# Chunked attention and token mixer on one core: stores on two queues and a new hand-ordered list

## The chip, the cores and the metric

The kernel runs on one core of a Trainium2 chip. The metric is the device time of one execution in microseconds (us). The kernel before takes 140.97 us (median of 3 runs, 140.26 to 141.21). One more execution was taken with the hardware profiler: it took 141.5 us, and its span, from the first to the last instruction of the program, is 139.7 us.

## The reference

Two layers follow each other. The first is attention inside chunks of 64 tokens (8 batches, 8 heads, 576 tokens of 64 values, so 9 chunks per head). The second is a token mixer without a softmax on the result, x, of the first.

```python
scores = scale * q_c @ k_c.T            # per chunk of 64 tokens and per head
attn   = exp(scores - max); attn /= sum + 1e-9
x      = (attn @ v_c)                   # -> [8, 576, 512]
wq, wk = x @ w_q, x @ w_k               # 512 -> 64
W_tok  = 1/8 * einsum('bsd,btd->bst', wq, wk)
mixed  = einsum('bst,btd->bsd', W_tok, x)
out    = relu(mixed) @ w_out            # float32 [8, 576, 512]
```

The kernel uses that `mixed = wq @ (wk.T @ x)`: it forms the small matrix G = wk.T @ x of a batch (64 x 512) and multiplies it with wq, so that no 576 x 576 matrix is made.

## The kernel before

**Units.** The tokens are cut into 20 units (`pairs`, lines 139 to 143). A whole unit has 256 tokens of one batch; a rest unit (u2, u7, u12, u17) has the last 64 tokens of two neighbouring batches. Units 18 and 19 are the two whole units of batch 7, unit 15 and 16 those of batch 6.

**Nodes.** Each unit goes through the same steps, each a `Node`: transposes of q and k on TensorE (`tq`, line 380), their copies out of PSUM (`qkt`: into `qbd` for q and `kt` for k), the scores S (line 400), maximum, subtraction and exponential (lines 413, 424, 434), transposes of the exponentials (line 446), attention times V (line 477), division (lines 491 to 505, giving `xs`), transposes of x (line 523), projections to wq and wk (line 533, `wt`), a transpose of wk (line 550). When both units and the rest of a batch are there, G follows (line 587, copied to `g16`), then for each unit the mix (line 627), the relu (`rm`, lines 645 and 647) and the output products (line 662), whose results are copied to `osb` in SBUF (line 313, through the helper `copy`) and stored to HBM. A copy out of PSUM can go to VectorE or ScalarE.

**The order.** Nothing is scheduled on the chip. `ORDER` (lines 69 to 104) is a list made offline, by a planner with costs for each node and landing times for each load. `12a` runs node 12 on ScalarE, `12v` on VectorE, `12p6` on TensorE with PSUM bank 6, and `i7.256` is an idle product: a product of ones with 256 columns into bank 7 (line 701) that nobody reads. The list is emitted from left to right (lines 697 to 706); each engine runs its own instructions in the order of emission and waits for semaphores where a node needs another one's result.

**Loads and stores.** The q and k of the first unit come by SyncE's queue as float32 (line 205) and are cast by four `cast` nodes, 0 to 3. All other loads are issued by GpSimd (lines 210, 213, 220, 227, 231, 234) in the order of `LOADS`, with a cast to float16 on the way. One item of that list, `clear`, zeroes the lower half of the three `g16` tiles with GpSimd memsets (line 238). All stores are issued by SyncE. While loads are still to be emitted, `store` keeps them in `held`; then SyncE issues a small DMA that reads the last value loaded of v (line 273), the held stores (line 275), and each later store as soon as its node is emitted (line 282). A whole unit's two stores (256 KB each, one for each half of the partitions) are emitted with the second of its two `osb` copies, a rest unit's two (128 KB each) with its only one; unit 19 has one store of 256 KB and two of 128 KB. That makes 41 stores.

The end of the list before is

```
... 612p0 605v 606p1 616p2 614p3 549p7 608p6 550v 609v 548a 621a 613a 607a 617a 615a
```

where 608 and 549 are the last two output products (second halves of units 18 and 16), 609 and 550 their copies, 548 the copy of the first half of unit 16, 621 that of rest unit 17, 613, 617 and 615 those of unit 19 and 607 that of the first half of unit 18.

Of the kernel before, what the change touches and what calls it, by code (L numbers as in the profile page):

```python
# [11 lines left out]
F32 = mybir.dt.float32  # L12
# [49 lines left out]
    "rm2": 4,  # L62
    "rm1": 2,
}
LOADS = "q1 v0 q2 clear v1 wqk v2 q3 q4 v3 q5 wo v4 q6 v5 q7 v6 q8 v7 q9 v8 q10 v9 q11 v10 q12 v11 q13 v12 q14 v13 q15 v14 q16 v15 q17 v16 q18 v17 q19 v18 v19"

ORDER = """
2v 3v 0a 1a i7.256 i6.256 i5.256 i7.256 i6.256 i5.256 i7.256 i6.256 i5.256 i7.256 i6.256 i5.256 i7.256 i6.256  # L70
i5.256 i7.256 i6.256 i5.512 i7.512 i6.512 i5.256 i7.256 4p0 6a 5v i7.512 i6.512 i5.512 i7.256 i6.256 7p1 8a
i7.512 i6.512 i5.512 i7.256 9p0 29p7 32p6 30a 33a 31a 10v 11v i5.512 i4.512 i3.512 i5.512 i4.512 i3.512 i5.256
i4.256 34p6 35v 12a i5.256 i4.256 i3.256 54p0 57a 56a 55a 13p1 i5.512 i4.512 i3.256 i5.256 i2.256 58p0 14a 36v
37a 59v i5.256 15p2 19p6 20v 60v 16v 21v i5.512 i4.512 38p1 17v 22v 18v 61a 39a i5.512 i4.256 62p0 63a i5.256
40p6 44p4 64p0 i3.512 89p2 23p3 41v 42v 45v 65v 66v 46v 67v 43v 47v 68p0 92p1 93v i7.256 48p4 90a 91a i5.256
i2.256 94p6 69v 114p2 i1.512 i0.256 117p5 95v 96v 49a 24a i4.256 25p3 50p4 70p0 26v 71v 51v 116a 115a 118a
119p6 27p5 i3.256 i2.256 52p4 97a 72p3 98p2 120v 73a 28a 53a 121v 158p5 99a 74p4.3 100p0 161p2 104p6 101v 102v
76v 105v 106v 103v 107v 159a 75a 160a 162a 122a 77p4 163p2 83p0 108p6 123p7 78a 84a 124a 164v 165v 81p4 79p5
129p2 125p0 85p7 166a 109v 110p6 80v 130v 86a 111a 183p5 112p6 186p7 126v 82v 131v 132v 127v 128v 185a 184a
113v 187v 133p4 134a 167p6 188p0 135p7 168a 136a 173p4 169p2 189v 137p7 208p6 138a 210a 209a 211a 87p7 212p6  # L80
174v 190v 170v 171v 172v 213v 214v 175v 176v 139p0.1 191a 88a 140a 141a 192p2 243p7 215a 142p0 216p6 177p3
148p4 244a 245a 178a 193v 217v 143v 218p6 246p2 149a 179p3 247a 180a 219v 220v 194p4 198p0 221v 195v 199v 196v
200v 197v 201v 248p6 268p3 271p2 270a 272a 181p4 222p5 202p0 223a 269a 249v 250v 203a 152p1 224p5 273p2 204p0
225a 251a 205a 146p5 226p6 153v 274v 227v 182v 252p1 206p0 275v 147a 312p7 315p6 253a 207a 228p0.1 254p2 258p4
229v 255v 259v 256v 260v 257v 261v 314a 316a 230a 313a 276a 144p6 317p0 231p2 277p7 237p4 318v 278v 145a 232a
238a 319v 150p6 340p7 337p2 283p0 279p4 341v 284v 280v 151v 281v 285v 282v 286v 233p3 320a 339a 338a 234a 321p7
362p6 154p4 262p2 364v 322v 342p0 365a 363a 263a 155a 287p3 239p7 288a 264p2 366p6 289p3 265a 240a 343v 344v
290v 345a 156p2 157a 266p3 291p7 235p0 346p1 292a 347a 267a 323p4 367v 368v 236v 369a 327p6 400p0 397p1 324v
328v 325v 329v 326v 330v 401a 399a 398a 293p3.2 295v 352p4 348p6 370p0 241p2 371a 242a 294v 349v 353v 350v 354v
351v 355v 302p0 402p6 303a 403v 331p2 356p3 332a 357a 372p4 422p0 425p2 373v 374v 375v 404v 423a 426a 424a  # L90
358p3 376p1 296p4 333p2 359a 377v 297v 334a 405a 308p6 427p0 378p2 428v 306p3 360p4 406p5 379a 309a 380p2 407v
310p6 335p7 361a 307a 381a 336a 408p4 412p2 466p7 429v 311a 469p6 494p0 491p1 413v 414v 409v 415v 410v 495v
411v 382p2.3 384v 383v 467a 468a 470a 430a 493a 492a 471p6 298p0 431p2 391p4 416p1 472v 473v 299a 432a 392a
300p0 433p6 437p2 417v 301a 438v 439v 434v 435v 440v 436v 516p1 496p4 304p0 474a 305a 518v 497v 385p2 386a
441p6 418p0 395p7 442a 475p2 419v 498v 519a 517a 396a 443p6 393p3 444a 420p6 445p7 520p4 499a 389p5 476v 500p2
394a 521v 421a 446a 501a 390a 522v 481p6 477p0 554p4 482v 478v 483v 479v 484v 480v 551p2 555a 553a 552a 447p5.3
448v 449v 506p6 502p0 485p4 507v 503v 508v 504v 505v 509v 456p2 387p5 556p0 523a 486a 457a 388v 450p6 451a
524p4 510p5 579p2 557v 576p3 525v 580a 578a 577a 558v 559a 526p6 527v 511v 528v 529v 487p2 458p4 581p0 512p5
582v 583v 459a 513a 462p6 530p3 560p4 488a 531a 561a 463a 514p5 460p2 532p4 489p3 562p6 566p0 567v 568v 563v
490v 564v 569v 565v 515a 533a 584a 534p4 452p5 535a 461a 585p3 586a 536p4.0 587p2 591p6 570p1 571a 537a 538v  # L100
588v 589v 592v 590v 593v 594v 464p0 572p1 539p2 595p4 540v 573a 596a 454p1 574p4 597p6 541p7 598a 575a 599p4
600a 453a 455v 465v 545p2 601p4.6 603a 602a 542a 546v 543p5 544a 618p2 610p0 547p4 619v 611v 604p2 620p5 612p0
605v 606p1 616p2 614p3 549p7 608p6 550v 609v 548a 621a 613a 607a 617a 615a
"""


# [1 line left out]
def kernel(  # L108
# [59 lines left out]
    def half(i):  # L168
        return slice(C * i, C * i + C)
# [63 lines left out]
    def load_wo():  # L233
        nc.gpsimd.dma_start(wo[:], moe_w_out.rearrange("(f p) n -> p f n", p=P))

    def clear():
        for t in g16:
            nc.gpsimd.memset(t[half(1), :], 0.0)

    load_qk(0)  # L240
    make_identity(nc, ident[:])
    arrive["f32", 0], arrive["f32", 1] = 4.85, 6.2
    loads = []
    for e in LOADS.split():
        u = int(e[1:]) if e[1:].isdigit() else None
        rest = u is not None and pairs[u][1] is None
        if e == "wqk":
            landing("w", 1.7)
            loads.append((load_w, [], None))
        elif e == "clear":  # L250
            loads.append((clear, [], None))
        elif e == "wo":
            landing("wo", 3.3)
            loads.append((load_wo, [], None))
        elif e[0] == "q":
            for t in range(2):
                landing(("qk", u, t), 0.94 if rest else wide)
            loads.append((load_qk, [u], None))
        else:
            landing(("v", u), halves if rest else 2 * halves)  # L260
            loads.append((load_v, [u], next((w for w in heir_v if heir_v[w] == u), None)))
# [4 lines left out]
    def load_more():  # L266
        while loads and made_v.get(loads[0][2], 0) == 2:
            load, args, _ = loads.pop(0)
            load(*args)
        if not loads and held:  # L270

            last = slot[len(pairs) - 1]
            nc.sync.dma_start(const.tile([1, 2], F16, name="held")[:], v_all[0:1, last + 1, H - 1, D - 2 : D])
            for to, of in held:
                nc.sync.dma_start(to, of)
            held.clear()

    def store(to, of):
        if loads or held:
            held.append((to, of))  # L280
        else:
            nc.sync.dma_start(to, of)

    load_more()

# [3 lines left out]
    def add(*a, **kw):  # L289
        n = Node(*a, **kw)  # L290
        nodes.append(n)
        return n
# [13 lines left out]
    def either(n):  # L306
        return {"ACT": act(n), "DVE": vec(n)}
# [12 lines left out]
    for t in range(2):  # L320
        for i in range(2):

            def ev(eng, t=t, i=i):
                to = qk[0][:, t, 4 * i : 4 * i + 4, :]
                copy(eng, to.rearrange("p h e -> p (h e)"), wide_in[t][:, i, :])

            cost = {"ACT": act(512, True), "DVE": 0.58}
            ready.setdefault(t, []).append(add("cast", cost, ev, [landed(("f32", t))]))

    def turns(u):  # L330
        b, m = pairs[u]
# [243 lines left out]
    def mixing(b):  # L575
# [21 lines left out]
        def ev_g(eng, c):  # L597
# [3 lines left out]
        deps = [st["wt_n", u] for u in mine + [rest]]  # L601
        n = add("G", {"PE": 5 * 0.11}, pe_g, deps, form=TALL, takes=bg, size=10)
        st["g_n", b] = [
            add("g16", either(DM // 2), lambda eng, c=c: ev_g(eng, c), [n], reads=bg[c])
            for c in range(2)
        ]
        for u in mine:
# [4 lines left out]
    def mix_out(u, batches):  # L612
# [41 lines left out]
        for i in range(ni):  # L654

            wide = DM // 2 if (b, m, i) == (B - 1, NPB - 1, 1) else DM
            for at in range(0, DM, wide):
# [12 lines left out]
                def ev_o(eng, i=i, bo=bo, s=s, wide=wide):  # L670
                    if not osb:
                        osb.append(home("osb", [P, 2, DM], F32))
                    copy(eng, osb[0][:, i, s], in_banks(bo, wide)[:, 0])
                    done.append(s)
                    if m is None:
                        for c in range(2):
                            store(out[b + c, S - C : S, :], osb[0][half(c), i, :])
                    elif turned(u, 1):
                        t0 = 2 * P * m + i * P
                        store(out[b, t0 : t0 + P, s], osb[0][:, i, s])  # L680
                    elif len(done) == 2:
                        rows = out[b, 2 * P * m : 2 * P * m + 2 * P, :].rearrange("(x p) d -> p x d", p=C)
                        for c in range(2):
                            store(rows[:, 1:3] if c else rows[:, 0:4:3], osb[0][half(c)])

                n1 = add("out", {"PE": wide / 512 * 0.864}, pe_o, [n, landed("wo")], form=FULL, takes=[bo], size=4)
                add("osb", either(wide), ev_o, [n1], reads=bo).pair = u
# [47 lines left out]
```

## Time and profile before

| what | value |
|---|---|
| time, median of 3 | 140.97 us |
| profiled execution: time, span | 141.5 us, 139.7 us |
| outside the span | 1.8 us |
| TensorE products busy | 123.1 us, 88% of the span |
| VectorE busy | 110.1 us, 79% |
| ScalarE busy | 99.9 us, 72% |
| GpSimd busy (issue of loads) | 75.9 us, 54% |
| end of the last product | 129.4 us |
| first and last issue of a store | 96.7 us, 135.7 us |

A busy TensorE is not one at its peak: matmuls are pipelined and their ends are modelled. Times in views of the trace are counted from the start of the span. A line of the timeline gives the start, the length, the engine, the source line, the operation and how many such instructions follow each other; in brackets the idle time of the engine before it and what ended it. "issue" is an idle time that ends without anything that the profile shows. "SPq" is SyncE's queue of DMA issues.

### The profile page before, as it was taken

What the parts mean: (1) busy time and instruction counts of PE and PEld (TensorE: products, weight loads), DVE (VectorE), ACT (ScalarE), POOL (GpSimd) and SP (SyncE); (2) the same over time, 40 slices, a digit from 0 to 9 for tenths busy, and PEclk for the clock granted to TensorE, in tenths of its full rate; (3) what the DMA queues carried; (4) which work ended last, traced back from release to release, by engine and by line L of the source; (5) the groups of instructions that cost most, each with busy time, mean ns of one, the idle gap of its engine ahead of it and who ended that gap; (6) DMA issues with size and microseconds to landing.
All of it is one profiled execution on the core that took longest, in us unless ns stands there. A gap on an engine that the chain in (4) does not pass through costs nothing.

```text
span 139.7 us, 5142 instructions
## 1 busy us (share of the span) xinstructions
PE 123.1 (88%) x2198; PEld 88.8 (64%) x2198; DVE 110.1 (79%) x212; ACT 99.9 (72%) x186; POOL 75.9 (54%) x99
## 2 busy tenths in 40 slices
PE   6999997988999979999999899999999999999000
PEld 4567566767476757767767778767778766555000
DVE  5358998697979998999999799999799978781200
ACT  6337854789678967999788798989998975655000
POOL 7999997835699986699987599800000000000000
PEclk9999999999999999999999999999999999999955
DMA  3999999999999999999999999991888878885583
GB/s 91 262 168 154 125 167 170 185 184 175 155 134 172 169 176 174 161 136 169 176 173 172 164 146 168 176 152 9 224 278 238 253 239 247 277 275 167 137 269 120
DMA packets 86250, 25.10 MB, mean 180 GB/s; under 512 B 78932, under 2 KB 81748, under 8 KB 86228
## 3 DMA queue, kind: packets, MB, share of 16 engines
q0 software_dynamic: 78752, 14.29, 126.6%
q1 hardware_dynamic: 7476, 10.49, 25.5%
q8 instruction: 17, 0.28, 0.8%
q14 instruction: 5, 0.04, 0.1%
HBM read 29.62 MB, written 9.44 MB: 280 GB/s over the span
## 4 chain that ended last, share of the span: by engine, by line
PE 66%; DVE 14%; ACT 8%; issue 5%; DVEq 0%
PE ps L662 18%; PE ps L380 10%; PE ps L701 8%; PE ps L400 5%; PE ps L523 5%; PE ps L533 5%; PE ps L477 4%; PE ps L627 4%; PE ps L446 4%; DVE mx L413 3%; DVE sh L424 3%; DVE xs L505 3%; PE ps L587 2%; ACT es L434 2%; ACT rm L647 1%
## 5 line engine op out<-in xcount | busy, mean ns | idle before, releaser
L662 PE MATMUL ps<-wo,rm 128*128 128x512 f16 (+1 forms) x148 | 36.0, 373 | 0.0
L227 POOL DMA_DIRECT2D v_all<-in_v_dram x33 | 29.0, 901 | 4.7 <-DMA qk<-in_q_dram 1.5
L313 ACT COPY qbd<-ps 64x512 f32<-64x512 f32 (+1 forms) x37 | 20.2, 546 | 9.0 <-PE ps L380 8.0
L413 DVE TENSOR_REDUCE mx<-ps 128x16 f32<-128x1024 f32 (+1 forms) x20 | 22.2, 1111 | 4.4 <-PE ps L400 4.1
L505 DVE TENSOR_TENSOR xs<-ps,rec 128x512 f16<-128x512 f32 x36 | 23.5, 681 | 0.3
L380 PE MATMUL ps<-ident,qk 128*64 128x128 f16 x512 | 18.8, 221 | 2.4 <-issue 2.0
L434 ACT ACTIVATE es<-sh 128x1024 f16<-128x1024 f32 (+1 forms) x20 | 19.5, 975 | 1.6 <-DVE sh L424 1.1
L662 PEld LDWEIGHTS <-rm 128*128 128x128 f16 x148 | 13.4, 98 | 10.2 <-issue 0.2
L424 DVE TENSOR_TENSOR sh<-ps,mx 128x1024 f32<-128x1024 f32 x16 | 19.6, 1224 | 0.3
L380 PEld LDWEIGHTS <-qk 128*64 128x64 f16 x512 | 15.3, 110 | 5.5 <-issue 3.6
L313 ACT COPY osb<-ps 128x512 f32<-128x512 f32 (+1 forms) x27 | 15.2, 570 | 4.2 <-PE ps L662 2.9
L701 PE MATMUL ps<-ones 128*128 128x256 f16 (+1 forms) x62 | 14.4, 369 | 1.2 <-DVE ones L155 1.2
L647 ACT ACTIVATE rm<-ps 128x1024 f16<-128x1024 f32 (+1 forms) x13 | 14.7, 1151 | 0.4 <-PE ps L627 0.4
L213 POOL DMA_DIRECT2D qk<-in_q_dram x15 | 13.7, 916 | 1.8 <-DMA qk<-in_k_dram 1.2
L213 POOL DMA_DIRECT2D qk<-in_k_dram x15 | 13.6, 904 | 0.7 <-DMA qk<-in_k_dram 0.5
L400 PEld LDWEIGHTS <-qbd 128*128 128x128 f16 x288 | 10.5, 98 | 2.5 <-ACT qbd L313 1.3
L400 PE MATMUL ps<-kt,qbd 128*128 128x64 f16 x288 | 11.7, 193 | 0.2 <-ACT kt L313 0.2
L446 PE MATMUL ps<-ident,es 128*128 128x128 f16 x144 | 11.4, 220 | 0.4 <-ACT es L434 0.2
L477 PE MATMUL ps<-v_all,et 64*64 64x65 f16 x576 | 9.9, 195 | 1.5 <-issue 1.1
L627 PE MATMUL ps<-wt,g 128*128 128x256 f16 (+1 forms) x96 | 11.1, 246 | 0.1
L523 PE MATMUL ps<-ident,xs 128*128 128x128 f16 x144 | 10.9, 219 | 0.3 <-DVE xs L505 0.3
L446 PEld LDWEIGHTS <-es 128*128 128x128 f16 x144 | 8.7, 98 | 3.6 <-ACT es L434 2.3
(56 smaller groups left out, 182.8 us busy)
## 6 DMA issues: line engine op xcount, KB each, us to landing
out_dram<-osb SPq DMA_DIRECT2D x31, 256.0 KB, 4.0
v_all<-in_v_dram POOLq DMA_DIRECT2D x31, 128.0 KB, 7.5
qk<-in_q_dram POOLq DMA_DIRECT2D x15, 256.0 KB, 7.0
qk<-in_k_dram POOLq DMA_DIRECT2D x15, 256.0 KB, 7.6
out_dram<-osb SPq DMA_DIRECT2D x10, 128.0 KB, 3.3
v_all<-in_v_dram POOLq DMA_DIRECT2D x10, 64.0 KB, 6.0
osb<-in_q_dram SPq DMA_DIRECT2D x1, 512.0 KB, 4.1
osb<-in_k_dram SPq DMA_DIRECT2D x1, 512.0 KB, 5.5
```

The costliest lines, as they stand in the source:

```text
L213: nc.gpsimd.dma_start(qk[u][:, t], rows)
L227: nc.gpsimd.dma_start(v_all[on, slot[u] + i, :, 0:D], v[b, :, of, :].rearrange("h p d -> p h d"))
L313: (nc.vector.tensor_copy if eng == "DVE" else nc.scalar.copy)(to, of)
L380: nc.tensor.transpose(tp[half(o), j, :, r, :], of, ident[:])
L400: nc.tensor.matmul(sp[:, i, j, c ^ turned(u, i), :], lhsT=st["qb", u][:, j, x].rearrange("p o s -> p (o s)"), rhs=st["kt", u][:, j, x * C ...
L413: nc.vector.tensor_reduce(mx[:], scores(), axis=AX.X, op=ALU.max)
L424: nc.vector.tensor_tensor(out=sh[:].rearrange("p x (g r) -> p x r g", r=R), in0=in_banks(bs, 512).rearrange("p i (x r g) -> p (i x) r g", ...
L434: nc.scalar.activation(es[:].rearrange("p x s -> p (x s)"), st["sh", u][:].rearrange("p x s -> p (x s)"), AF.Exp, scale=scale_attn,)
L446: nc.tensor.transpose(ep[:, x, :], es[:, x, :], ident[:])
L505: nc.vector.tensor_tensor(out=to, in0=xp()[:, :, :, 0:D], in1=by, op=ALU.mult)
L662: nc.tensor.matmul(in_banks(bo, wide)[:, 0], lhsT=st["rm", u][:, f, i * P : i * P + P], rhs=wo[:, f, s], start=(f == 0), stop=(f == NF - 1),)
L701: nc.tensor.matmul(ps[:, at[0], 0 : at[1]], lhsT=ones[:, 0:P], rhs=ones[:, 0 : at[1]], start=True, stop=True)
```

## The change

Five things change.

1. `store` takes the issuing engine. Of the two stores of a whole unit (but unit 19) and of a rest unit, the first half of the partitions goes by SyncE, the second by GpSimd. Unit 19's three stay on SyncE. So 22 stores are on SyncE, 19 on GpSimd. They are held in the same way; only SyncE issues the small DMA first.
2. `clear` leaves the list of loads. Three new nodes, numbered 4 to 6, zero the lower halves of `g16` on VectorE or ScalarE; the first copy into each of these tiles depends on them. All later nodes get a number higher by 3.
3. The planner's landing time of the first k goes from 6.2 to 6.65 us. What the planner knows of the instruction blocks is not in the kernel: it shows only in the list.
4. `ORDER` is a new list: other places, banks and engines for many nodes.
5. Idle products: 40 of 256 columns and 22 of 512 become 21 of 256 and 31 of 512, so 21,504 columns become 21,248. The first block, before any transposes, has 5,120 columns (6,400 before), and 4,096 (2,048 before) stand between the transposes of the first q and those of the first k.

In the new list all three `clear` nodes are on ScalarE, and of the casts of the first unit one q cast is on VectorE and three casts on ScalarE (before: q on ScalarE, k on VectorE).

```diff
-LOADS = "q1 v0 q2 clear v1 wqk v2 ...
+LOADS = "q1 v0 q2 v1 wqk v2 ...
...
-2v 3v 0a 1a i7.256 i6.256 i5.256 i7.256 ...
...
-605v 606p1 616p2 614p3 549p7 608p6 550v 609v 548a 621a 613a 607a 617a 615a
+1a 0v i7.512 i6.512 i7.512 i6.512 i7.512 i6.512 i7.512 i6.512 i7.512 i6.256 i5.256 7p0 2a 3a i7.512 i6.512
+i5.512 i7.512 i6.512 i5.512 i7.512 i6.256 i5.256 10p1 8v 9a i7.256 32p0 34v 11a 33a i5.256 12p6 13v 14v 35p1
...
+613p6 614a 621p2 550p5 622v 607p0 623p4 615p6 608v 609p7 619p0 617p1 552p2 611p3 612v 553v 551a 624a 616a 610a
+620a 618a
...
-            for to, of in held:
-                nc.sync.dma_start(to, of)
+            for by, to, of in held:
+                by.dma_start(to, of)
...
-    def store(to, of):
+    def store(by, to, of):
         if loads or held:
-            held.append((to, of))
+            held.append((by, to, of))
         else:
-            nc.sync.dma_start(to, of)
+            by.dma_start(to, of)
...
+    def ev_clear(eng, to):
+        if eng == "DVE":
+            nc.vector.memset(to, 0.0)
+        else:
+            nc.scalar.mul(to.bitcast(F32), ones[half(1), :].bitcast(F32), 0.0)
...
-            add("g16", either(DM // 2), lambda eng, c=c: ev_g(eng, c), [n], reads=bg[c])
+            add("g16", either(DM // 2), lambda eng, c=c: ev_g(eng, c), [n] + clear.get(b, []), reads=bg[c])
...
-                            store(out[b + c, S - C : S, :], osb[0][half(c), i, :])
+                            store((nc.sync, nc.gpsimd)[c], out[b + c, S - C : S, :], osb[0][half(c), i, :])
...
-                            store(rows[:, 1:3] if c else rows[:, 0:4:3], osb[0][half(c)])
+                            store((nc.sync, nc.gpsimd)[c], rows[:, 1:3] if c else rows[:, 0:4:3], osb[0][half(c)])
```

At the end of the new list, 611 and 552 are the last two output products (second halves of units 18 and 16), 612 and 553 their copies, 551, 624, 616, 610, 620 and 618 the copies that were 548, 621, 613, 607, 617 and 615.

More of the change, by code (lines that the diff above doesn't have):

```diff
@@ L64 @@
 }
-LOADS = "q1 v0 q2 clear v1 wqk v2 q3 q4 v3 q5 wo v4 q6 v5 q7 v6 q8 v7 q9 v8 q10 v9 q11 v10 q12 v11 q13 v12 q14 v13 q15 v14 q16 v15 q17 v16 q18 v17 q19 v18 v19"
+LOADS = "q1 v0 q2 v1 wqk v2 q3 q4 v3 q5 wo v4 q6 v5 q7 v6 q8 v7 q9 v8 q10 v9 q11 v10 q12 v11 q13 v12 q14 v13 q15 v14 q16 v15 q17 v16 q18 v17 q19 v18 v19"
 ORDER = """
-2v 3v 0a 1a i7.256 i6.256 i5.256 i7.256 i6.256 i5.256 i7.256 i6.256 i5.256 i7.256 i6.256 i5.256 i7.256 i6.256
-i5.256 i7.256 i6.256 i5.512 i7.512 i6.512 i5.256 i7.256 4p0 6a 5v i7.512 i6.512 i5.512 i7.256 i6.256 7p1 8a
@@ L72 @@
[L72 to L101, printed above, removed]
@@ L102 @@
-600a 453a 455v 465v 545p2 601p4.6 603a 602a 542a 546v 543p5 544a 618p2 610p0 547p4 619v 611v 604p2 620p5 612p0
-605v 606p1 616p2 614p3 549p7 608p6 550v 609v 548a 621a 613a 607a 617a 615a
+1a 0v i7.512 i6.512 i7.512 i6.512 i7.512 i6.512 i7.512 i6.512 i7.512 i6.256 i5.256 7p0 2a 3a i7.512 i6.512
+i5.512 i7.512 i6.512 i5.512 i7.512 i6.256 i5.256 10p1 8v 9a i7.256 32p0 34v 11a 33a i5.256 12p6 13v 14v 35p1
+36a i5.512 i4.512 i3.512 i5.256 i4.256 37p0 i5.512 i4.512 i3.512 i5.512 i7.256 57p6 38v 39v 15a 58a 59a 60a
@@ new lines @@
+i5.512 i4.256 16p7 17a 40a i5.512 i4.256 61p6 i5.256 22p0 62v 23v 24v 63v 25v i5.512 i4.512 i3.512 i5.256 41p7
+i3.256 18p4 19v 42a i3.512 i2.256 47p6 43p2 20v 21v 48v 64a i1.256 65p0 26p1 66a 27a 4a i0.256 67p4 92p0 44v
+49v 50v 45v 46v 68v i7.256 28p1 51p2 95p3 52a 69v 93v 70v 94v i7.256 i6.256 71p4 96a 72v 29a 53p2 54v 97p6 98v
+30p3 73p4 55p2 74a i5.512 i1.256 75p4 i0.512 117p5 120p0 118v 99v 56a 31a 76a 121a 119a 77p4.1 122p2 161p5 78a
+123v 100a 79a 101p4 163a 86p0 164p6 102a 162a 124v 165v 103p2 87a 107p4 104v 105v 108v 106v 109v 110v 80p6
@@ new lines @@
+166p0 88p2 167v 125a 81a 126p3 111p4 84p5 89a 127a 112a 168v 132p2 128p6 113p4 186p0 133v 129v 134v 135v 114v
+169a 187a 188v 130v 189p1 131v 190a 115p4 170p2 191p0 136p3 82p6 171a 85a 137a 138p5 139a 116a 192v 193v 194a
+211p7 176p2 213v 214v 172p0 140p4 173v 174v 212v 177v 175v 178v 179v 83a 5a 141a 195p5 215p7 196a 142p4.6 201p0
+197p2 246p5 216v 202v 203v 204v 198v 199v 217v 143a 144a 249p6 180p4 90p0 200v 181v 247a 248a 250a 218a 6a 91a
+251p6 145p2 205p1 219p0 182p4 146a 271p5 274p2 252v 253v 220a 183a 206a 275a 254a 151p6 272v 273v 221p0 222v
@@ new lines @@
+223v 207p4 276p2 255p5 224v 152a 225p0 208v 184p1 209p4 226v 277v 315p6 318p0 185a 256a 227p5 155p1 317a 316v
+319a 228a 229p5 320p6 149p0 230a 156a 278v 210a 321v 231p1.4 340p5 279a 280p2 343p3 232a 233a 150a 322v 257p6
+261p0 258v 262v 259v 263v 260v 264v 147p4 342a 281a 344a 341a 157p2 234p6 235v 148a 158a 323a 265p5 345p0 346v
+240p2 266a 153p4 286p6 347v 241a 365p5 324p2 367a 366a 368a 154v 287v 288v 325v 267p3 268v 289v 242p0 236p1
+243a 237a 282p2 326p4 330p6 283v 284v 327v 328v 285v 403p0 400p1 402v 369p2 370v 331v 290p3 348a 404a 371v
@@ new lines @@
+159p0 291a 401a 292p3 372a 293a 269p1 238p2 294p3 332v 160v 329v 373p0 270a 333v 374v 239a 405p4 295a 349p1
+296p0.3 375p6 334p2 297a 350a 298a 335a 406v 407v 376v 408a 244p0 311p4 305p2 377v 306a 245v 378v 312v 428p1
+425p0 469p6 429a 351p2 355p4 427v 352v 356v 353v 357v 358v 354v 336p1 313p7 426a 337a 470a 314a 471v 379p4
+299p0 380a 300a 359p5 360v 430p2 338p4 381p6 382v 409p7 361p5 383p6 362a 410a 384a 309p0 363p5 339v 431v 432v
+472p4 364a 385p5.1 497p6 386v 387v 310a 473a 433a 498a 411p2 415p4 416v 412v 413v 417v 414v 303p7 304v 418v
@@ new lines @@
+394p0 519p6 474p2 434p7 520v 395a 419p4 388p0 435a 522a 420a 475v 521v 476v 301p7 421p6 389a 494p4 436p2 440p0
+422v 437v 441v 438v 439v 442v 443v 302a 496a 495a 523p5 423p7 307p6 424v 477a 499p2 398p4 478p7 444p0 500v 501v
+399a 479a 308v 445a 396p4 484p0 480p2 502a 446p7 397a 447a 392p6 503p4 393a 448p7 449a 485v 481v 524v 525v 486v
+482v 487v 483v 504a 554p5 450p7.6 557p4 509p2 505p0 451v 452v 555a 558a 556a 526a 510v 506v 511v 507v 512v 508v
+390p6 559p4 459p2 488p7 527p0 391a 560v 579p6 582p1 460a 528v 561v 529p2 580a 583a 489a 530v 531v 581v 513p0
@@ new lines @@
+453p4 461p1 584p6 532v 514v 562a 585v 586v 454a 563p2 533p0 462a 534a 564a 515p3 463p4 465p0 535p2 490p5 466a
+516a 536a 569p6 565p0 464v 570v 491v 517p4 537p2 455p3 538v 571v 518v 566v 567v 572v 568v 587a 492p2 588p4 493a
+589a 539p2.5 590p6 594p0 591v 595v 596v 592v 593v 597v 541a 573p5 540a 574a 467p2 542p4 575p6 598p7 576a 599a
+457p0 600p1 577p7 578a 543v 456v 458v 601a 544p3 602p1 603a 548p6 604p1.0 546p4 549v 547v 545a 606a 605a 468a
+613p6 614a 621p2 550p5 622v 607p0 623p4 615p6 608v 609p7 619p0 617p1 552p2 611p3 612v 553v 551a 624a 616a 610a
@@ L234, in load_wo @@
         nc.gpsimd.dma_start(wo[:], moe_w_out.rearrange("(f p) n -> p f n", p=P))
-    def clear():
-        for t in g16:
-            nc.gpsimd.memset(t[half(1), :], 0.0)
     load_qk(0)
     make_identity(nc, ident[:])
-    arrive["f32", 0], arrive["f32", 1] = 4.85, 6.2
+    arrive["f32", 0], arrive["f32", 1] = 4.85, 6.65
     loads = []
@@ L249 @@
             loads.append((load_w, [], None))
-        elif e == "clear":
-            loads.append((clear, [], None))
         elif e == "wo":
@@ L328 @@
             ready.setdefault(t, []).append(add("cast", cost, ev, [landed(("f32", t))]))
+    clear = {}
+    def ev_clear(eng, to):
[3 more added lines that the diff above has]
+            nc.scalar.mul(to.bitcast(F32), ones[half(1), :].bitcast(F32), 0.0)
+    for n, t in enumerate(g16):
+        cost = {"ACT": act(256, True), "DVE": 0.28}
+        clear[n] = [add("clr", cost, lambda eng, t=t: ev_clear(eng, t[half(1), :]), ready[0])]
     def turns(u):
@@ L676, in ev_o @@
                         for c in range(2):
-                            store(out[b + c, S - C : S, :], osb[0][half(c), i, :])
+                            store((nc.sync, nc.gpsimd)[c], out[b + c, S - C : S, :], osb[0][half(c), i, :])
                     elif turned(u, 1):
                         t0 = 2 * P * m + i * P
-                        store(out[b, t0 : t0 + P, s], osb[0][:, i, s])
+                        store(nc.sync, out[b, t0 : t0 + P, s], osb[0][:, i, s])
                     elif len(done) == 2:
```

## The prediction

> **What bounds the kernel now.** I read the span by stages first. In the stage table the columns are the busy time of each engine with its count of instructions, then the granted clock, the DMA share and GB/s.
>
> ```profile
> 8.00:24.00 16.00, 15.27 (x310) 10.86 (x307) 13.05 (x26) 9.64 (x17) 15.60 (x20) 1.00 2.03 155
> 24.00:56.00 32.00, 28.55 (x564) 21.34 (x565) 27.78 (x53) 25.15 (x47) 24.01 (x30) 1.00 1.94 169
> 56.00:96.00 40.00, 39.22 (x785) 29.88 (x783) 37.96 (x75) 35.59 (x65) 29.09 (x36) 1.00 1.99 157
> 96.00:126.00 30.00, 29.87 (x485) 20.92 (x483) 26.00 (x51) 23.68 (x51) 0.00 (x0) 1.00 0.80 239
> 126.00:140.00 14.00, 3.41 (x20) 1.76 (x18) 1.38 (x2) 1.80 (x4) 0.00 (x0) 0.75 0.57 168
> ```
>
> TensorE (first pair of columns, products) is idle 0.73 + 3.45 us between 8 and 56 us, 0.78 us from there to 96 us, and 0.13 us in the 30 us after that. The loads end long before it does, so TensorE's queue, in the order of the list, sets when the last product ends. After that comes a tail without products. Next, the waits: who waited for what, us in total, times, longest.
>
> ```profile
> PE ps L380 <- issue: 2.0, 2, 1.1
> PE ps L477 <- issue: 1.1, 2, 0.6
> ACT osb L313 <- DMA out_dram<-osb: 1.0, 2, 0.7
> ...
> SPq L282 <- DVE osb L313: 3.4, 1, 3.4
> ```
>
> Of TensorE's 4.2 us of idle time from 8 to 56 us and what little follows, 3.1 us in four waits end on nothing that the profile shows ("issue"). In the trace they stand 256 TensorE instructions or a multiple of that apart (instructions 706, 962, 1729 and 2753), and each ends 1.3 to 1.6 us after the end of one of the 17 packets of 16 KB in the queue of instructions: the code is late. The last line is SyncE's store queue: it had no more to do and waited 3.4 us for one VectorE copy. That copy is in the last view, the timeline of the end.
>
> ```profile
> 124.06 5.35 PE L662 MATMUL ps<-wo,rm 128*128 128x512 f16 x28
> ...
> 128.58 0.69 DVE L313 COPY osb<-ps 128x512 f32<-128x512 f32 x1 [3.00 <-PE ps L662]
> 129.34 7.18 SPq L282 DMA_DIRECT2D out_dram<-osb  x9
> 129.50 0.69 DVE L313 COPY osb<-ps 128x512 f32<-128x512 f32 x1 [0.23 <-PE ps L662]
> ```
>
> The last product ends at T = 129.4. The copy 550 ends at 129.27, and then SyncE issues nine stores in a row. Only unit 16's and unit 18's four needed a copy that late; the five of units 17 and 19 were ready between 125.7 and 128.1 but are behind unit 16's in the queue. From the first of the nine to the end of the span it is 139.7 - 129.34 = 10.36 us. So the kernel is T plus a store tail of 10.3 us.
>
> **The change part by part.** The sum goes against the profiled execution: span 139.7, time 141.5, so 1.8 us lie outside. Its time is 0.5 us over the median of the runs, 140.97, and I take that off at the end. About 1% (1.4 us) is what a measurement of this kernel can tell from no change.
>
> *Loads and clear.* The three GpSimd memsets (1.6 us, L238, at 7.9 to 9.5 us) go, so the loads behind them are issued 1.6 us sooner. But each of these lands 4 to 7 us after its issue because the DMA engines are already busy with earlier ones: the share is 2.03 in that stage. They land no sooner; worth 0, at best a few tenths for v1. On ScalarE three clears of 64x256 float32 come in; the nearest row is the qbd copy of that shape, 371 ns, so 1.1 us in the whole list; a g16 tile is first written after 30 us, so they have room.
>
> *Start.* Twenty idle blocks of 256 columns at the 213 ns spacing that the trace shows in the first 6 us end at 1.20 + 4.27 = 5.5. The q casts now run side by side, from 4.91 to 5.53 on ScalarE (616 ns) and to 5.6 on VectorE (707 ns): the q transposes start near 5.7, not 6.64. The k transposes gain nothing: k lands at 6.72, its two casts end on ScalarE at 6.75 + 1.23 = 8.0 (8.08 before on VectorE), and the 4,096 idle columns ahead of them, at the 216 ns per 512 seen after 7 us, take 1.73 us after transposes of 0.6 to 1.2 us: 8.0 to 8.6, against 8.19 before. I take +0.15; ends -0.2 and +0.4.
>
> *Idle products.* Behind that start nothing but 256 columns in all is saved, so 0.1 to 0.2 us. I take -0.15. "Fewer" means no less time on TensorE.
>
> *VectorE and ScalarE.* By rows, VectorE gets 12 more qbd halves (668 ns), 2 + 1 small ones of rest units (0.43, 0.41), one osb copy and one small rm (0.69 each) and 2 wt (0.42), and gives up one cast (0.71), 4 et (0.68), 5 g (0.42), 3 kt (0.68) and 2 rm (1.29): +1.3 us in 110. ScalarE comes to +0.3 us with the clears. Both stay below TensorE; 0 on the end by itself.
>
> *The list.* Real products are the same in number and shape. What can change is TensorE's idle time from 8 to 96 us: 4.2 + 0.8 us. The four code waits (3.1 us) are not removed by a planner that knows of them; it can only put other work around them. The rest up to 56 us, 1.1 us, are waits for copies (E for the exponential, xT for xs, and so on). I compared how much TensorE work lies between each producer and its user in both lists (scores to E, E to V, x to its transposes, G to mix): the distances are alike, a little longer for scores to E, shorter for wk to G. I take half of 1.1 us: -0.5. The ends: all 4.2 us gone, or as much again in new waits as in the 24 to 56 stage (+3).
>
> *The end of the list.* After G of the last batch TensorE has the same products in both lists, so T moves only with the above. But copy 612, of the very last product, is now emitted before 553. VectorE runs 612 from T + 0.1 to T + 0.8, then 553 to T + 1.5 (two copies of 0.69). Unit 16's stores wait for 553, and six on SyncE and three on GpSimd start with these. First issue: T + 1.55 instead of T - 0.07, **+1.6 us**.
>
> *Two queues.* The nine stores carry 1.84 MB.
>
> ```profile
> 121.00:125.00 4.00, 4.00 (x35) 2.27 (x30) 3.40 (x4) 2.29 (x5) 0.00 (x0) 1.00 0.88 272
> 129.30:133.30 4.00, 0.11 (x1) 0.00 (x0) 0.69 (x1) 0.00 (x0) 0.00 (x0) 0.96 0.63 155
> 133.30:138.60 5.30, 0.00 (x0) 0.00 (x0) 0.00 (x0) 0.00 (x0) 0.00 (x0) 0.50 0.72 230
> L282 SPq DMA_DIRECT2D out_dram<-osb x35: 537/693/1708, 102.1 to 135.7; - x35
> ```
>
> Over the drain they move at 230 GB/s at a share of 0.72 (8.0 us for 1.84 MB); in the middle one queue reaches 272 GB/s at 0.88. The bounds: no gain, if the engines behind the queue are the limit (landings of two 256 KB stores in the tail are 1.1 to 1.2 us apart though their issues are 0.65 apart); or SyncE keeps its own pace with three stores less, 3 x 0.8 us, plus what overlaps: -2.7. A third bound goes below nothing: a GpSimd store may land late. GpSimd issues take 0.69 to 0.90 us, its three end their issue by T + 4, and medians from issue to landing on its loaded queue are 4.4 to 7.6 us, so at worst T + 11. I take the rate of the nearest row, 272 GB/s: 6.75 us, -1.2. Earlier stores gain nothing: SyncE's queue had run empty (the 3.4 us wait), and ScalarE's 1.0 us for free `osb` buffers lies beside a run of 28 products without a gap.
>
> Row against rule: the trace has SyncE issuing faster than stores land. The Trainium skill, page "DMA: Bandwidth & Descriptors", section "Issuing engines are not separate DMA queues", says that DMAs issued from several engines interleave on the same 16 DMA engines, and that only the issue time is saved; by this rule the -1.2 would be nearly 0, which is the second rival.
>
> **Sum:** +0.15 - 0.15 - 0.5 + 1.6 - 1.2 = -0.1 us; 141.5 - 0.1 - 0.5 = 140.9. I forecast **140.9 us**, no change.
>
> **The rivals.**
> *The list waits less* (faster). For it: 4.2 us of idle TensorE before 56 us, and none after 96. If half goes (-2.1) and the tail at least breaks even, 138.9; with the tail's best end 137.8. Against: code waits stay, and the distances are alike.
> *The tail gets longer* (slower). One mechanism: the first store starts 1.6 us later and the two queues drain 1.84 MB no faster than one. Then it is 140.97 + 1.6 - 0.5 = 142.1 with the list's gain, 142.6 without. It decides as soon as the drain gains less than 0.3 us or so. For it: landings slower than issues. That is also the case in which the split doesn't do what it says.
> *New waits in the list* (slower): GpSimd's stores follow its loads at once, from 90 us, and code packets share the DMA engines; each late block costs 0.5 to 1.15 us, and any wait after 56 us is paid in full since nothing is idle there. Two or three of them: 143.
>
> **How the numbers follow.** Forecast, within 1.4 us of 140.97: 0.40. Faster list: 0.32. Longer tail 0.18 and new waits 0.10, which come out over 1% slower: 0.28. The range leaves out a tenth on each side: 138.2 to 143.1; the likeliest case's own is 139.6 to 142.4.
>
> **What would show it.** Of the next profile: the end of the last product at 128.9 +- 1; two VectorE copies after it, 0.7 us each; the first of the last nine stores at T + 1.55 on both queues; from there to the end 9.2 us (10.4 if the engines limit, under 8 if not); TensorE's idle time from 8 to 56 us near 3.7 us with three to five waits on "issue". The k transposes of unit 0 at 8.0 to 8.6. I would be wrong if T moved by more than 1.5 us, or if the tail were not between 9.2 and 11.9 us after T.

## The result and the profile after

The changed kernel takes 146.65 us (median of 4 runs, 145.68 to 146.93) against 141.09 us for the kernel before beside it: 1.0384 times the time, 95% interval 1.0309 to 1.0459. It is slower by 5.6 us, where I had forecast no change and a range up to 143.1. Its profiled execution took 145.68 us with a span of 143.9 us, so the two profiles differ by 4.2 us of span. The rest is spread between executions: the profiled one of the kernel before took 0.4 us more than the median beside it, that of the changed kernel 1.0 us less. Single runs of the kernel before go from 139.5 to 144.9 us over the chips, and executions more than 1.5% above the fastest of their kernel are left out of the ratios.

The first view is the stage table of the changed kernel (busy time and count for TensorE products, weight loads, VectorE, ScalarE, GpSimd; then granted clock, DMA share, GB/s).

```profile
8.00:24.00 16.00, 15.87 (x293) 10.85 (x294) 12.12 (x24) 8.30 (x17) 13.89 (x17) 1.00 2.03 156
24.00:56.00 32.00, 28.59 (x610) 22.29 (x605) 29.35 (x55) 27.56 (x51) 23.89 (x30) 1.00 1.89 163
56.00:96.00 40.00, 39.09 (x764) 29.06 (x764) 37.26 (x73) 34.55 (x67) 31.94 (x42) 1.00 2.06 171
96.00:126.00 30.00, 29.52 (x490) 20.93 (x489) 27.57 (x56) 23.44 (x44) 6.15 (x11) 1.00 0.80 218
126.00:144.00 18.00, 5.67 (x33) 2.93 (x30) 2.58 (x3) 3.10 (x7) 2.57 (x5) 0.80 0.54 146
```

From 8 us on TensorE is idle for 0.13 + 3.41 + 0.91 + 0.48 us. That is what it was before (0.73 + 3.45 + 0.78 + 0.13). So neither the new list's middle nor its waits made the kernel slower. What is left is the start and the tail. The waits of the changed kernel (us in total, times, longest) name the start:

```profile
PE ps L707 <- DVE ones L159: 4.5, 1, 4.5
```

And the timeline of its first microseconds shows what TensorE waited for:

```profile
0.86 0.27 DVE L155 MEMSET ones<- 128x256 f16 x1 [0.86 <-PEq L725]
1.19 0.10 PEld L707 LDWEIGHTS <-ones 128*128 128x128 f16 x1 [1.19 <-DVE ones L155]
...
4.13 0.27 DVE L159 MEMSET ones<- 128x256 f16 x1
4.45 3.65 PE L707 MATMUL ps<-ones 128*128 128x512 f16 x11 [4.45 <-DVE ones L159]
```

The `ones` tile is filled in two halves: columns 0 to 255 by VectorE's first memset (line 155), columns 256 to 511 by its last (line 159), behind the memsets of `v_all`, `qbd` and `wkr`. An idle product of 256 columns reads only the first half. The old list begins with those, at 1.20 us. The new list begins with `i7.512`, which reads all 512 columns, so TensorE loads its weights at 1.19 and then stands still until 4.45. The same view of TensorE alone, before and then after:

```profile
1.20 5.51 PE L701 MATMUL ps<-ones 128*128 128x256 f16 x22 [1.20 <-DVE ones L155]
6.64 0.65 PE L380 MATMUL ps<-ident,qk 128*64 128x128 f16 x16
7.22 1.04 PE L701 MATMUL ps<-ones 128*128 128x512 f16 x5
8.19 0.64 PE L380 MATMUL ps<-ident,qk 128*64 128x128 f16 x16
```

```profile
8.04 0.64 PE L386 MATMUL ps<-ident,qk 128*64 128x128 f16 x16
8.61 1.90 PE L707 MATMUL ps<-ones 128*128 128x512 f16 x9
10.44 0.64 PE L386 MATMUL ps<-ident,qk 128*64 128x128 f16 x16
```

The idle products must all be run before the q transposes, since the queue is in order. These come at 8.04 instead of 6.64, and the k transposes, behind more idle products, at 10.44 instead of 8.19: 2.25 us late. That is less than the 3.25 us by which the first idle product is late. Fewer columns stand ahead of the q transposes, and they ran faster: TensorE begins at 427 ns for 512 columns and later needs 216 ns, with a granted clock of 1.00 over the first 8 us. In this execution the pace changed 2.7 us after the first product, with a part of the first block still to run; in the profile of before it changed only at the end of the block, about 5 us after. The last product ends at T = 131.67 instead of 129.41: 2.26 us late. The rest of the 4.2 us is in the tail:

```profile
130.43 1.24 PE L668 MATMUL ps<-wo,rm 128*128 128x512 f16 x5
...
131.71 1.29 DVE L307 COPY osb<-ps 128x512 f32<-128x512 f32 x2 [3.90 <-PE ps L668]
133.06 7.32 SPq L276 DMA_DIRECT2D out_dram<-osb  x6
133.54 1.73 POOL L276 DMA_DIRECT2D out_dram<-osb  x3 [6.70 <-issue]
```

Both VectorE copies stand behind the last product, and the first of the last nine stores is issued at 133.06 = T + 1.39 (T - 0.07 before): +1.46 us. From there to the end it takes 143.9 - 133.06 = 10.8 us, against 10.4 before: +0.4 us. Start 2.3, first store 1.5 and drain 0.4 make the 4.2 us.

### The profile page after: what moved, and what is told of

It reads as the page before. It is cut to its first block, busy times and chain, and to the rows that moved or that the text cites. A ratio compares the mean times of both kernels' runs of the same rounds, so it can differ in the third digit from the quotient of the medians.

```text
span 143.9 us, 5131 instructions
## 1 busy us (share of the span) xinstructions
PE 122.3 (85%) x2188; PEld 87.5 (61%) x2188; DVE 112.0 (78%) x216; ACT 101.0 (70%) x185; POOL 85.5 (59%) x115
## 4 chain that ended last, share of the span: by engine, by line
DMA 36%; POOL 17%; DVE 16%; PE 13%; issue 10%; ACT 1%; POOLq 0%; DVEq 0%; ACTq 0%
DMA v_all<-in_v_dram 19%; DMA qk<-in_k_dram 17%; POOL qk L213 10%; PE ps L668 5%; DVE mx L419 4%; DVE sh L430 3%; POOL v_all L227 3%; POOL v_all L220 3%; DVE xs L511 3%; PE ps L633 2%; PE ps L539 1%; PE ps L593 1%; PE ps L529 1%; DVE g L307 1%; DVE qbd L307 1%
## 5 line engine op out<-in xcount | busy, mean ns | idle before, releaser
L276 POOL DMA_DIRECT2D out_dram<-osb x15 | 8.7, 586 | 31.0 <-DVE osb L307 8.8
L511 DVE TENSOR_TENSOR xs<-ps,rec 128x512 f16<-128x512 f32 x36 | 24.0, 684 | 0.5
L668 PEld LDWEIGHTS <-rm 128*128 128x128 f16 x148 | 13.3, 98 | 10.4 <-issue 0.4
L653 ACT ACTIVATE rm<-ps 128x1024 f16<-128x1024 f32 (+1 forms) x14 | 17.1, 1219 | 1.5 <-PE ps L633 1.4
L307 ACT COPY osb<-ps 128x512 f32<-128x512 f32 (+1 forms) x26 | 14.7, 568 | 3.6 <-PE ps L668 3.2
L707 PE MATMUL ps<-ones 128*128 128x512 f16 (+1 forms) x52 | 13.3, 369 | 4.5 <-DVE ones L159 4.5
L307 DVE COPY qbd<-ps 64x512 f32<-64x512 f32 (+1 forms) x17 | 10.5, 620 | 6.6 <-PE ps L386 6.2
L307 ACT COPY qbd<-ps 64x512 f32<-64x512 f32 (+1 forms) x23 | 12.5, 542 | 3.3 <-DVE qbd L307 2.4
L406 PEld LDWEIGHTS <-qbd 128*128 128x128 f16 x288 | 10.6, 98 | 3.5 <-ACT qbd L307 1.2
L307 ACT COPY kt<-ps 128x512 f32<-128x512 f32 (+1 forms) x18 | 10.0, 553 | 2.3 <-PE ps L386 2.2
```

What stands on the lines that cost most here:

```text
L307: (nc.vector.tensor_copy if eng == "DVE" else nc.scalar.copy)(to, of)
L406: nc.tensor.matmul(sp[:, i, j, c ^ turned(u, i), :], lhsT=st["qb", u][:, j, x].rearrange("p o s -> p (o s)"), rhs=st["kt", u][:, j, x * C ...
L511: nc.vector.tensor_tensor(out=to, in0=xp()[:, :, :, 0:D], in1=by, op=ALU.mult)
L653: nc.scalar.activation(to, of, AF.Relu, scale=scale_moe)
L668: nc.tensor.matmul(in_banks(bo, wide)[:, 0], lhsT=st["rm", u][:, f, i * P : i * P + P], rhs=wo[:, f, s], start=(f == 0), stop=(f == NF - 1),)
L707: nc.tensor.matmul(ps[:, at[0], 0 : at[1]], lhsT=ones[:, 0:P], rhs=ones[:, 0 : at[1]], start=True, stop=True)
```

## The experiments

Each is compared with runs of the kernel before on its own chip, so across chips the ratios are to be set side by side, not the times. A point is 0.01 of such a ratio, 1.4 us.

**The ones tile at once** (on the changed kernel).

```diff
-    nc.vector.memset(ones[:, 0:256], 1.0)
+    nc.vector.memset(ones[:], 1.0)
...
-    nc.vector.memset(ones[:, 256:512], 1.0)
```

> The changed kernel with all 512 columns of the ones tile set by VectorE's first memset instead of by its first and its last. In the changed kernel the first idle product (512 columns) starts at 4.45 us, after the last memset, where the kernel before started one of 256 columns at 1.20. Theory 'late start': this alone moved the k transposes of unit 0 from 8.19 to 10.44 and the last product T from 129.4 to 131.7. Then here the first idle product starts near 1.5, the k transposes near 8.4, T is 129.5 +- 0.5 and the time falls by 1.8 to 2.4 us against the changed kernel. Rival 'list': T is late because of the new list's waits from 24 to 56 us (3.4 us of idle TensorE in both kernels); the start is swallowed by later waits for loads: T falls by less than 0.7 us.

Measured: 143.57 us, ratio 1.0209 (1.0157 to 1.0262), against 1.0384 for the changed kernel: 1.75 points, 2.5 us. TensorE's timeline in it:

```profile
1.46 4.45 PE L706 MATMUL ps<-ones 128*128 128x512 f16 x11 [1.46 <-DVE ones L155]
5.84 0.65 PE L385 MATMUL ps<-ident,qk 128*64 128x128 f16 x16
6.42 1.90 PE L706 MATMUL ps<-ones 128*128 128x512 f16 x9
8.26 0.64 PE L385 MATMUL ps<-ident,qk 128*64 128x128 f16 x16
```

The transposes are at 5.84 and 8.26, T is at 129.51, and TensorE's idle time from 24 us on is the changed kernel's within 0.1 us. Late start holds; the rival, that later waits swallow it, falls. It also says that the new list is, apart from start and tail, as good as the old one in the profile of before: T 129.51 against 129.41. What still separates this kernel from the one before is its tail, 12.2 us against 10.3.

**The late start alone, in the kernel before.**

```diff
-2v 3v 0a 1a i7.256 i6.256 i5.256 i7.256 ...
+2v 3v 0a 1a i7.512 i5.256 i7.256 ...
```

> The kernel before with its first two idle products of 256 columns made one of 512, and nothing else: the same 6,400 columns ahead of the first transposes. Theory 'late start': it waits for VectorE's last memset and starts at 4.45 instead of 1.20 us, the q and k transposes of unit 0 come 2.2 to 3.2 us later, T with them, and the time rises by 2.2 to 3.2 us (143.3 to 144.3). Rival 'the late start costs only in the new list', whose idle products after it are many: under 1 us.

Measured: 144.43 us, ratio 1.0272 (1.0227 to 1.0318), 3.5 us over the kernel before beside it. One wide idle product at the head of the old list is enough:

```profile
4.46 5.22 PE L701 MATMUL ps<-ones 128*128 128x512 f16 x21 [4.46 <-DVE ones L159]
9.62 0.64 PE L380 MATMUL ps<-ident,qk 128*64 128x128 f16 x16
...
11.15 0.64 PE L380 MATMUL ps<-ident,qk 128*64 128x128 f16 x16
```

The k transposes are 2.96 us late and T is 132.8, 3.4 us late. It costs more here than in the changed kernel, and a little more than the 2.2 to 3.2 us expected. 6,400 idle columns stand before the q transposes instead of 5,120, which is 1.1 us at 427 ns for 512, and TensorE kept that pace for 4.8 us instead of 2.7. The last 0.45 us of T go with longer waits on "issue" (3.6 us in all, 3.1 before). The rival (under 1 us) falls.

**The two last copies in the other order** (on the changed kernel).

```diff
-... 611p3 612v 553v 551a ...
+... 611p3 553v 612v 551a ...
```

> The changed kernel with the copies 612 and 553 emitted in the other order (553, ready one product sooner, first). Theory 'the first store of the tail sets the end': 553 ends near T - 0.1 instead of T + 1.3, the first of the nine stores is issued 1.4 us sooner, and the time falls by 1.4 us. Rival 'the drain is bound by what comes last' (unit 18's stores need 612, which ends at T + 0.7 either way): less than 0.5 us.

Measured: 145.32 us, ratio 1.0322 (1.0269 to 1.0376), 0.6 points or 0.9 us below the changed kernel's ratio; the intervals overlap. In its profile the first of the nine stores is issued at 132.63 = T - 0.1, and the tail is 10.9 us instead of 12.2: 1.3 us shorter, as the first theory said. Its T is later by 1.0 us (132.71). Half of that is the start: the first q transposes of that execution came 0.5 us later still, at 8.57, since TensorE's pace changed 3.8 us after the first product. The other half goes with one wait of 0.6 us on "issue", which the changed kernel's profile doesn't have. So the tail's share is shown by the profile; the time alone does not decide it.

**All stores on SyncE** (on the changed kernel).

```diff
-store((nc.sync, nc.gpsimd)[c], ...
+store(nc.sync, ...
```

> The changed kernel with all 41 stores on SyncE again. From the first of the last nine stores to the end of the span it took 10.36 us before and takes 10.84 in the changed kernel, with SyncE's last two issues at 2.0 and 2.3 us (0.6 to 1.1 before). Theory 'two queues are no faster': with one queue the drain is 10.4 us again, the time falls by about 0.5 us, and SyncE's issues from 97 to 105 us go from about 2 us back to 0.6 to 1.2. Rival 'two queues help, something else made the tail long': the drain grows by 1.2 us or more, to 12 us.

Measured: 146.06 us, ratio 1.0375 (1.0319 to 1.0431): no difference from 1.0384 that these runs can tell. In the profile the drain is 10.6 us instead of 10.8, and SyncE's issues are as short as before. Its T is 0.5 us later (132.17), here too with one wait of 0.6 us on "issue". The two lines are the stores emitted one by one, with min/median/max of an issue in ns, first in the changed kernel, then here:

```profile
L276 SPq DMA_DIRECT2D out_dram<-osb x18: 557/1020/2286, 105.0 to 138.1; - x18
```

```profile
L276 SPq DMA_DIRECT2D out_dram<-osb x33: 537/637/1578, 102.0 to 139.9; - x33
```

With half the stores, SyncE's median issue is 1.02 us instead of 0.64. The split takes stores off SyncE's queue and makes those left longer. The drain by stages, changed kernel first (the last two columns are DMA share and GB/s):

```profile
133.00:138.00 5.00, 0.00 (x0) 0.00 (x0) 0.00 (x0) 0.00 (x0) 1.73 (x3) 0.89 0.70 173
138.00:142.60 4.60, 0.00 (x0) 0.00 (x0) 0.00 (x0) 0.00 (x0) 0.00 (x0) 0.50 0.72 211
```

```profile
133.50:138.50 5.00, 0.00 (x0) 0.00 (x0) 0.00 (x0) 0.00 (x0) 0.00 (x0) 0.85 0.66 181
138.50:142.80 4.30, 0.00 (x0) 0.00 (x0) 0.00 (x0) 0.00 (x0) 0.00 (x0) 0.50 0.71 216
```

Two queues move 173 and 211 GB/s where one moves 181 and 216. The rival, a drain of 12 us on one queue, falls.

**The split alone, in the kernel before.** The edit is the part of the change in `store` and its callers.

> The kernel before with the stores split over SyncE and GpSimd, and nothing else. Theory 'two queues are no faster': T stays at 129.4, the drain from the first of the last nine stores is 10.4 to 10.9 us, the time is 0 to 0.5 us above the kernel before. Rival, as predicted: the drain falls to 9.2 us and the time by 1.2 us. If GpSimd's stores from 90 us on delay the code of TensorE, T is later by 0.5 us or more.

Measured: ratio 1.0113 (1.0023 to 1.0204), so slower by 0.2 to 2%, from three executions. In its profile the drain is 10.9 us, 0.5 us over the kernel before, and SyncE's median issue is 1.09 us (0.69 before). T was 127.8 in that execution, 1.6 us earlier than in the profile of before. Its k transposes started at 7.50, but so they did in the next run below, whose T is 129.55. Of the four profiles of the old list only this one has few waits on "issue", 0.4 us instead of 3.1 to 3.6; a wait of 1.0 us for a load of q took a part of that back. My predicted gain of 1.2 us from two queues is not there. That GpSimd's stores delay TensorE's code isn't seen either: idle time after 96 us is 0.12 us.

**The tail of the kernel before in the order in which copies end.**

```diff
-... 550v 609v 548a 621a 613a 607a 617a 615a
+... 548a 621a 613a 607a 617a 615a 550v 609v
```

> The kernel before with the copies 550 and 609 emitted last instead of ahead of 548, 621, 613, 607, 617 and 615, so that SyncE issues the five stores of units 17 and 19 as their copies end (125.7 to 128.1 us) and only the four of units 16 and 18 after T. Theory 'queue order sets the tail': T stays at 129.4; four stores from T - 0.1 at 0.7 to 0.8 us each, landing 3 to 4 us later, end near T + 6.5: the time falls by 3.5 to 4 us, to 137.3. Rival 'the DMA engines set the tail': 1.84 MB at 230 GB/s from 125.8 us on end no sooner than 133.8 + 1.1, and contention makes that later: a fall of 2 us or less.

Measured: 139.50 us, ratio 0.9898 (0.9833 to 0.9964): 1.4 us faster. The tail is 8.0 us instead of 10.3, T the same (129.55). The five stores of units 17 and 19 are issued from 127.13 to 130.0, though ready from 125.85, since stores of earlier units are still ahead of them in the queue. These five, and then the last four:

```profile
127.13 3.27 SPq L282 DMA_DIRECT2D out_dram<-osb  x5
130.49 3.18 SPq L282 DMA_DIRECT2D out_dram<-osb  x4
```

So the gain is 2 us or less, as the rival said. That the DMA engines set this limit isn't shown by this run, in which SyncE also issues almost without a pause from 125 us to the end of its issues.

**All three mended, on one queue** (the changed kernel).

```diff
-... 611p3 612v 553v 551a 624a 616a 610a 620a 618a
+... 611p3 551a 624a 616a 610a 620a 618a 553v 612v
```

with the ones tile set at once and all stores on SyncE.

> The changed kernel with the ones tile set at once, all stores on SyncE, and the copies 553 and 612 emitted last, in that order, behind 551, 624, 616, 610, 620 and 618. If start and tail are all that is wrong with the changed kernel and its list is as good as the old one: T at 129.5, a tail of 6 to 7 us, the same time as the kernel before with its tail put in order (137 to 138). If the new list costs something of its own, T is 130.5 or later.

Measured: 138.66 us, ratio 0.9864 (0.9807 to 0.9921), faster than both kernels. T is 129.2, so the new list costs nothing of its own; the tail is 7.9 us, longer than the 6 to 7 expected and as long as in the old list put in order (8.0). The end of its timeline:

```profile
129.26 0.69 DVE L306 COPY osb<-ps 128x512 f32<-128x512 f32 x1 [0.17 <-PE ps L667]
129.95 3.03 SPq L275 DMA_DIRECT2D out_dram<-osb  x4
```

**The same on two queues.**

> As the run with all three mended, but with the stores split over SyncE and GpSimd. Theory 'two queues are no faster': 0 to 0.6 us over that run, with SyncE's last issues at 1 us or more. Rival 'with few stores at the end two queues help': two stores on each queue after T, 0.7 us sooner than with four on one.

Measured: 139.69 us, ratio 0.9939 (0.9906 to 0.9971). Against the one with the ones tile alone (1.0209) the order of the tail is worth 2.7 points, 3.8 us, more than the 1.5 us that the first store costs: the five stores that had been stuck behind unit 16's now go out before T. Against the run on one queue, on the same chip, the split costs 1.0 us in the median, though the two intervals overlap a little.

I had expected long last issues on SyncE, 1 us or more. They take 0.6 us, and the last store lands at 135.80 us, no later than on one queue (135.99). The profile shows another wait, in GpSimd's closing instructions. These lines (POOLq is GpSimd's, SPq SyncE's) have the count, the min/median/max in ns, and the first and last start.

```profile
L735 POOLq DRAIN  x3: 51/93/5950, 131.3 to 137.7; - x3
L735 SPq DRAIN  x3: 7/7/7, 136.2 to 137.5; - x3
```

The longest `DRAIN` of GpSimd runs from 131.28 to 137.23, 1.4 us past the landing of its last store. SyncE is through with its own at 136.3, and the span ends at 138.0. In the changed kernel GpSimd's `DRAIN` also ended 1.4 us after its last landing (142.47 after 141.03), but SyncE's last store landed at 142.52, so that it cost nothing there. The two mended profiles differ by 0.9 us of span, and SyncE was through 0.95 us before GpSimd. That this wait is the whole of the 1.0 us in the times is not shown: there is one profile on two queues, and its start was slower as well (k transposes at 8.80 against 7.83, T at 130.0 against 129.2).

**The same on one queue, once more, and with two of the last four stores from ScalarE.**

```diff
-store(nc.sync, rows[:, 1:3] if c else ...
+store((nc.sync, nc.scalar)[c if u in (16, 18) else 0], rows[:, 1:3] if c else ...
```

> The changed kernel with all three mended (ones tile at once, all stores on SyncE, copies 553 and 612 last), once more, as the base for the next run: 138 to 139 us, tail 7.9 us.

> The kernel with all three mended, and of the last four stores (units 16 and 18) the two of the second partition half issued by ScalarE, which has no work left then, instead of SyncE. Theory 'the DMA engines are the limit, whichever queue issues': the last store is issued 1.3 us sooner, but lands within 0.5 us of where it did; the time changes by less than 0.5 us. Rival 'a queue's issue is the limit, only GpSimd's kind of queue is slow': tail 7.9 to 6.7 us, the time falls by 1.2 us.

Measured: 138.45 us, ratio 0.9836 (0.9789 to 0.9883), for the repeat, whose interval lies below that of the two-queue version (0.9906 to 0.9971). Its tail was 6.9 us, not the 7.9 expected: in the first of the two profiles SyncE was still issuing earlier stores when copy 553 ended and came to unit 16's 0.9 us later, in this one at once. With ScalarE's queue 138.76 us, ratio 0.9853 (0.9804 to 0.9903): no gain. A limit in SyncE's issue would have given 1.2 us. There is no profile of an execution of that length, so where its stores landed can't be read. The argument rests on the times: they exclude a gain of 1.2 us from SyncE's issue, and do not show by themselves that the DMA engines are the limit.

## Why the prediction was wrong

**Start: the step that failed.** The prediction put the first twenty idle blocks from 1.20 us on, at 213 ns each, and came to +0.15 us. It measured 2.25 us at the k transposes and 2.26 us at T. The rest of the step was sized well: with the ones tile set at once, the transposes stand at 5.84 (5.7 predicted) and 8.26 (8.0 to 8.6 predicted), though VectorE's q cast took 0.43 us in the changed kernel where I had 0.71. The spacing holds only until the pace changes, and when that is differs by execution. What I had not asked was what the first product reads. I counted columns and took 512 as twice 256; but the width also chose the producer. The profile of before had it all: the first idle product waits for line 155, and line 159 ends at 4.40.

```profile
0.87 0.27 DVE L155 MEMSET ones<- 128x256 f16 x1 [0.87 <-PEq L719]
4.13 0.27 DVE L159 MEMSET ones<- 128x256 f16 x1
```

The delay is paid in full: in seven profiles of the new list T comes 121.2 to 121.8 us after the k transposes, which stand anywhere from 7.83 to 10.98. No rival had this either, so the range missed.

**The list.** I took -0.5 us of waits. TensorE's idle time from 8 to 56 us came to 3.54 us, near the 3.7 predicted, but not as predicted: I kept the four waits on "issue" as fixed, and the changed kernel has none of them. Waits for copies took their place (0.74 us for `qbd`, 0.63 us for an exponential). The term also rested on a slip: one of the four waits (0.58 us at 79.3) lies behind 56 us, so before it 1.7 us and not 1.1 were left for other waits. With the start mended T is at 129.2 to 130.0 in four profiles, against 129.4 before (and 127.8 for the old list with few waits on "issue"), so the runs show no gain where I had -0.5.

**Idle products, VectorE, ScalarE, clear.** -0.15 us and zeros. VectorE's busy time rose by 1.9 us (I had 1.3) and ScalarE's by 1.1 (0.3). No run tests these terms one by one; T with the start mended, within 0.1 us of that of before in the first such profile, gives no sign against them.

**The end of the list.** Predicted: first store at T + 1.55. Measured: T + 1.39. The mechanism and the size held, and swapping the two copies took 1.3 us out of the tail again.

**Two queues.** Predicted -1.2 us, with 0 as one bound. Measured +0.4 us in the changed kernel, +0.5 us in the split alone, and 1.0 us of time between the two mended versions, where GpSimd's closing `DRAIN` ends last. I took the 272 GB/s that one queue reaches in the middle for the rate that two reach at the end; they reach 173 to 211 GB/s, as one does. In the tail the second rival's mechanism, a later first store and two queues that drain no faster, is what the profile shows: 12.2 us, where I had set 11.9 as the bound. The rule of the Trainium skill ("DMA: Bandwidth & Descriptors", "Issuing engines are not separate DMA queues") was the better guide than my row. Here it even understates: not only is nothing but issue time saved, SyncE's own issue time rises from a median of 0.64 us to 1.02 us (from 0.66 to 0.74 us in the mended kernel).

**The sum.** Of the 4.2 us of span 2.3 are the start, 1.5 the first store and 0.4 the drain. In times the runs give 1.75 points for the start, 2.7 for the order of the tail (more than the change had added, since the order before was not good either) and 0.75 for the split, on the way from 1.0384 to 0.9864. That the times of the changed kernel lie 5.6 us over those of before, and its profile only 4.2, is because the two profiled executions lie on opposite sides of their medians, by 0.4 and 1.0 us. What made them do so, no run settles.

## What to carry to other kernels

Before a filler or a warm-up instruction is made wider, look at what it reads and who writes that last: a product that nobody needs still waits for its operands, and an in-order queue makes everything behind it wait as well. In a queue of stores, the one emitted first decides for all: emit in the order in which data get ready, and look at the emission order of the copies when they run on two engines. A second issuing queue is worth trying only where the trace shows the first one issuing without a pause while the DMA engines have room; stores that land further apart than they are issued (here 1.1 to 1.2 us against 0.65) are the sign that they have not. Look also at when the second engine is through: GpSimd needed 1.4 us after its last store had landed.

## What the runs showed that I had not expected

The waits of TensorE on "issue", which I had read as a fixed 3.1 us of late code, are not fixed. They were 3.1 us in the profile of before, 3.6 and 3.2 us in two variants of it, but 0.4 us in the one with split stores, and 0 to 0.8 us in the changed kernel and in six profiles of its variants. Its total idle time from 24 to 56 us stayed at 3.4 to 3.6 us all the same. Whether that is due to where the blocks of code end in the list, or to what the loads do at that moment, no run here tells.

And a second queue lengthens the issues of the first: SyncE's median issue of the stores emitted one by one went from 0.69 us to 1.09 us in the kernel before when GpSimd issued half of the stores, with single ones up to 2.8 us. In the mended kernel it went only from 0.66 to 0.74 us.

The first products of TensorE run at half the later pace, and how long they do isn't set by the list: 2.7 us after the first product in the changed kernel, 2.9 and 3.0 in two profiles of the kernel mended on one queue, 4.8 in the old list with the late start, and more than 5 in the one mended on two queues, all at a granted clock of 1.00. With the same list and the same start the k transposes came at 7.83, 7.91, 8.26 and 8.80. So two single profiles of this kernel can differ by 1 us before any change is at work.
